# One list of fine steps for the start: attention of tiles 0 to 2 and the first layer of tiles 0 and 1

## The chip, the core and the metric

The kernel runs on one core of a Trainium2 chip. The time is that of the whole kernel on the device in microseconds (us), from inputs in HBM to the output in HBM; lower is better. Five queues run side by side, each in its own order: TensorE (PE, its weight loads as PEld), VectorE (DVE), ScalarE (ACT), GpSimd (POOL) and SyncE (SP), which here only issues DMAs. An instruction waits for semaphores of other queues, and all that stands behind it on its queue waits too.

## What is computed

Windowed causal attention over 4 batches, 8 heads, 576 positions and 64 columns, then two feed-forward blocks, all in float32:

```python
scores = scale * np.matmul(q, k.transpose(0, 1, 3, 2))
mask = (rel >= 0) & (rel < 64)                       # rel = row position - column position
scores = np.where(mask, scores, -1000000000.0)
scores = scores - np.max(scores, axis=-1, keepdims=True)
attn = np.exp(scores)
attn = attn / (np.sum(attn, axis=-1, keepdims=True) + 1e-09)
x = np.matmul(attn, v)                               # then laid out as 2304 tokens x 512
h = x @ moe_w_in;  x = (np.maximum(h, 0.0) + alpha * np.minimum(h, 0.0)) @ moe_w_out
h = x @ moe2_w_in; out = (h * (1.0 / (1.0 + np.exp(-h)))) @ moe2_w_out
```

The two inner widths are 2048. Weights arrive as 64-bit floats and are turned into float32 on DVE by bit operations.

## The kernel before

The 2304 tokens are cut into six tiles of 384. Attention is done in **items**: item n is two heads (128 rows of q and k) of one tile, four items a tile, so items 0 to 3 are tile 0, 4 to 7 tile 1, 8 to 11 tile 2. The steps of an item:

- S, `mm_s` (L178): 24 small matmuls into two PSUM banks, half "a" and half "b".
- softmax of a half (L188): three DVE instructions (L199) that add the mask and find the row minimum of the negated scores, then three ACT exponentials (L204).
- `rescale` (L210): DVE adds 1e-9 to the sums (L218), takes the reciprocal (L219) and multiplies the half by it in one instruction of 128x384 (L222).
- T, `mm_t` and `keep_t`: three PE transposes a half (L230), and one ACT copy of the bank to SBUF (L237).
- P, `mm_v` and `keep_v`: 24 matmuls with v (L247), an ACT copy rounded to the fast float format (high part, L256) and a DVE subtraction (low part, L257).

The first layer of a tile is 16 **chunks** f of 128 hidden rows. A chunk's weights are loaded by SP (L265) into one of four staging buffers, converted by three DVE instructions (L276, L279, L282), copied to a high part by ACT (L289) and subtracted to a low part by DVE (L290). M, `mlp_h1` (L338), is then 12 matmuls of 128x384 into bank 0 or 1 in turn; G, `mlp_g1`, is two ACT reads of that bank (L345, L346), and one tile-chunk later DVE joins the two (L356) and SP stores the result (L368). M of tile t needs the high and low parts of all four items of that tile.

The order of each queue is that in which the program calls the steps. Two places call them here. First a hand-written list, `START` (L20), whose words stand for coarse steps: `s3a` is S of item 3, softmax of its half a and rescale of the half b before it; `s3b` is softmax of half b and rescale of half a; `t3a` is transposes and copy; `p3` is P with both parts; `w`, `c`, `h` with a number load, convert or split all chunks up to that number; `M` and `G` are for tile 0. The list ends after M and G of four chunks of tile 0. Then the loop over t (L935) begins with t = 1: it works on the items of tile 2 and does M and G of chunk f for tiles 0 and 1 (tile 1 alone for f below 4), with the next chunks' load, conversion and split behind them. From t = 2 on one tile is left for each t, and a plan brings in the weights of later layers.

Attention has PSUM banks 2 to 7, given out in fixed turn (`turn_ab`, L123); the probabilities of items below 8 have eight rooms in fixed turn (L121), the transposed ones two rooms (L122).

Of the kernel before, what the change touches and what calls it, by code (L numbers as in the profile page):

```python
# [20 lines left out]
q0 w1 s0a q1 q2 s0b w2 s1a v0 s1b c1 q3 s2a v1 z s2b t0a t0b h1 q4 s3a p0 v2 w3 s3b t1a t1b c2 p1 v3 q5 s4a w4 s4b  # L21
t2a t2b h2 v4 p2 s5a w5 s5b t3a t3b v5 p3 c3 w6 s6a t4a t4b s6b M0 p4 h3 G0 c4 s7a t5a t5b s7b M1 p5 w7 G1 h4 t6a t6b
s8a M2 p6 s8b c5 G2 t7a t7b M3 p7 h5 G3
# [8 lines left out]
def attention_two_mlps(ctx, tc, q, k, v, w_in1, w_out1, alpha, w_in2, w_out2, out):  # L32
# [92 lines left out]
    def att_bank():  # L125
        return bank(turn_ab(), "pa")
# [51 lines left out]
    def mm_s(n):  # L178
        it = items[n]
        it["sc"] = [att_bank()[:, :HB * P].rearrange("p (b c) -> p b c", b=HB) for _ in range(2)]  # L180
        for jb in range(NB):
            o = jb * W
            for e in range(2):
                r = slice(e * W, (e + 1) * W)
                nc.tensor.matmul(it["sc"][jb % 2][side(jb, e), jb // 2, :], it["qT"][r, o:o + W],  # L185
                                 it["kT"][r, o:o + P], start=True, stop=True)

    def softmax(n, hf):  # L188

        it = items[n]  # L190
        t = n // NHP
        sc = it["sc"][hf]
        pr = room(turn_early() if n < EARLY else turn_pr(), [P, HB, P], F32, "pr")
        if hf == 0:
            it["sm"] = sml.tile([P, 2 * HB], F32, name="sm")

        nm = sml.tile([P, HB], F32, name="nm")
        for j in range(HB):
            nc.vector.tensor_tensor_reduce(  # L199
                out=pr[:, j, :], in0=sc[:, j, :],  # L200
                in1=mask[:, min(1, (t * NB + 2 * j + hf) % (S // W))].rearrange("p u w -> p (u w)"),
                scale=-scale, scalar=3.0e38, op0=ALU.add, op1=ALU.min, accum_out=nm[:, j:j + 1])
        for j in range(HB):
            nc.scalar.activation(out=pr[:, j, :], in_=pr[:, j, :], func=AF.Exp,  # L204
                                 bias=nm[:, j:j + 1], scale=-1.0, accum_out=it["sm"][:, hf * HB + j:hf * HB + j + 1])
        it[f"p{hf}"] = pr
        if hf and n >= NHP:
            load_qk(n + 2)

    def rescale(n, halves=(0, 1)):  # L210
        it = items.get(n)
        if it is None or halves[-1] in it.setdefault("scaled", set()):
            return
        it["scaled"].update(halves)
        c = slice(halves[0] * HB, (halves[-1] + 1) * HB)
        sm = it["sm"][:, c]
        rs = sml.tile([P, 2 * HB, 1], F32, name="rs")
        nc.vector.tensor_scalar_add(sm, sm, 1e-9)  # L218
        nc.vector.reciprocal(rs[:, c, :].rearrange("p b o -> p (b o)"), sm)  # L219
        for hf in halves:  # L220
            pr = it[f"p{hf}"]
            nc.vector.tensor_tensor(out=pr, in0=pr, in1=rs[:, hf * HB:(hf + 1) * HB, :].to_broadcast([P, HB, P]),  # L222
                                    op=ALU.mult)

    def mm_t(n, halves=(0, 1)):
        it = items[n]
        for hf in halves:
            pb = it[f"b{hf}"] = att_bank()
            for j in range(HB):
                nc.tensor.transpose(pb[:, j * P:(j + 1) * P], it[f"p{hf}"][:, j, :], ident)  # L230

    def keep_t(n, halves=(0, 1)):

        it = items[n]
        for hf in halves:
            pt = it[f"pt{hf}"] = room(turn_pt(), [P, HB, P], F32, "pt")
            nc.scalar.copy(pt, it[f"b{hf}"][:, :HB * P].rearrange("p (b c) -> p b c", b=HB))  # L237

    def mm_v(n):
        it = items[n]  # L240
        pb = it["pv"] = att_bank()
# [8 lines left out]
    def keep_v(n):  # L250
        pb = items.pop(n)["pv"]
# [4 lines left out]
        nc.scalar.copy(xh, pb[:, :TN])  # L256
        nc.vector.tensor_tensor(out=xl, in0=pb[:, :TN], in1=xh.bitcast(F32), op=ALU.subtract)  # L257
        xt[t, hp] = (xh, xl)
        if n >= NHP:
            load_v(n + 2)  # L260

# [5 lines left out]

    def to_f32(s, a=None):
        a = a or cv.tile([P, DM], U32, name="cva", tag="cv")
        for k in range(3):  # L270
            f32_step(s, a, k)
        return a.bitcast(F32)
# [27 lines left out]
    def plain_steps(key, src, f, base):  # L300
        def load():
            held[key, f] = stage(src, f)

        def convert():
            held[key, f] = to_f32(held[key, f])

        def split():
            a = held.pop((key, f))
            wh, wl = (wroom((base + 2 * f + i) % 64, [P, DM], F32R, key) for i in range(2))
            parts(a, wh, wl)  # L310
            wt[key, f] = (wh, wl)
        return load, convert, split
# [28 lines left out]
    def mlp_g1(t, f):  # L341
# [5 lines left out]
        join_g1()  # L347
        halves.append((t, f, a, g))

    halves = []  # L350

    def join_g1():
        if not halves:
            return
        t, f, a, g = halves.pop()
# [370 lines left out]


    in1 = [plain_steps("i1", w_in1, f, 0) for f in range(KF)]
    done = {}

    def upto(chunks, step, n):
        k = (id(chunks), step)
        while done.get(k, 0) < min(n, len(chunks)):
            chunks[done.get(k, 0)][step]()
            done[k] = done.get(k, 0) + 1

    ahead = set()
    for w in START.split():
        rests()
        x, n = w[0], int(w[1:].rstrip("ab") or 0)  # L740
        if x in "qv":
            (load_qk if x == "q" else load_v)(n)
        elif x == "z":
            alpha_in()
        elif x == "s":
            if w[-1] == "a":
                mm_s(n)
                softmax(n, 0)
                rescale(n - 1, (1,))
            else:  # L750
                softmax(n, 1)
                rescale(n, (0,))
        elif x == "t":
            hf = (int(w[-1] == "b"),)
            rescale(n, hf)
            mm_t(n, hf)
            keep_t(n, hf)
        elif x == "p":
            mm_v(n)
            keep_v(n)  # L760
        elif x in "wch":
            upto(in1, "wch".index(x), n)
        else:
            (mlp_h1 if x == "M" else mlp_g1)(0, n)
            ahead.add(n)
# [169 lines left out]
    for t in range(1, NTILE):  # L935
        for f in range(KF):
            rests()
            n = (t + 1) * NHP + f // 4
            if t + 1 < NTILE:
# [3 lines left out]
                elif f % 4 == 0:  # L943
# [4 lines left out]
                    if n > EARLY:  # L948
                        rescale(n)
                        mm_t(n)  # L950
                    if f:
                        keep_v(n - 1)
                    if n > EARLY:
                        keep_t(n)
# [4 lines left out]
                elif f % 4 == 2:  # L959
                    if n == EARLY:  # L960
                        for hf in ((0,), (1,)):
                            rescale(n, hf)
                            mm_t(n, hf)
                            keep_t(n, hf)
                    rescale(n + 1)
            for tt in ((0, 1) if t == 1 and f not in ahead else (t,)):
                mlp_h1(tt, f)
                mlp_g1(tt, f)
            if t == 1:
                upto(in1, 1, f + 4)  # L970
                upto(in1, 0, f + 7)
                upto(in1, 2, f + 3)
            else:
                hook((t - NTILE) * KF + f)
# [9 lines left out]
    join_g1()  # L984
# [99 lines left out]
```

## Time and profile before

| | us |
|---|---|
| median of three runs | 846.58 (846.17 to 849.41) |
| the profiled execution, whole | 849.5 |
| its span, first to last instruction | 847.7 |
| PE busy | 811.8 (96%) |
| DVE busy | 643.8 (76%) |
| ACT busy | 509.5 (60%) |

The page gives the busy time of each engine over the span; a PE time is modelled, so that a wait between two matmuls can hide in it. The granted TensorE clock is shown as a share of full speed: 1.00 is 2.4 GHz and 0.50 is 1.2 GHz, and its mean over the span is 0.979. The chain of waits is followed back from the last instruction; the timeline shows instructions with their start, their length, and in brackets the idle time of the engine before them.

### The profile page before, as it was taken

How to read it: one execution, taken by the hardware profiler on the slowest of the kernel's cores; microseconds unless marked ns; L12 is line 12 of the kernel's file. 1: busy time of each engine (PE TensorE's matmuls, PEld its weight loads, DVE VectorE, ACT ScalarE, POOL GpSimd, SP SyncE). 2: the span in 40 equal slices, each digit the busy share in tenths (PEclk: the TensorE clock that was granted, in tenths of full speed). 3: DMA queues.
4: the chain of work that ended last, by engine and by line, in shares of the span. 5: the costliest groups of instructions: out<-in, count | busy, mean ns of one | idle time of the engine just before them, and what ended most of it. 6: DMA issues, size and time to landing. Idle time of an engine off the chain costs nothing.

```text
span 847.7 us, 17779 instructions
## 1 busy us (share of the span) xinstructions
PE 811.8 (96%) x5976; PEld 791.5 (93%) x5976; DVE 643.8 (76%) x1603; ACT 509.5 (60%) x1327; POOL 79.8 (9%) x108
## 2 busy tenths in 40 slices
PE   4689999999999999999999999999989999999998
PEld 3579999989899999999999989999989999999998
DVE  5678886879888899798899786664765887756754
ACT  4576665666665577565577646645656575554553
POOL 1000000000000014023122000000000030421410
PEclk9599999999999999999999999999999999999999
DMA  8457737786867789898999597585878889659631
GB/s 260 151 171 235 237 113 235 238 279 222 276 204 254 235 269 194 252 305 216 321 240 250 182 329 261 207 287 187 255 264 265 283 176 328 142 110 318 118 61 57
DMA packets 136844, 190.47 MB, mean 225 GB/s; under 512 B 13872, under 2 KB 122928, under 8 KB 136752
## 3 DMA queue, kind: packets, MB, share of 16 engines
q1 hardware_dynamic: 124080, 172.02, 62.2%
q0 software_dynamic: 12672, 17.31, 12.4%
q8 instruction: 47, 0.77, 0.4%
q14 instruction: 45, 0.37, 0.1%
HBM read 110.11 MB, written 61.87 MB: 203 GB/s over the span
## 4 chain that ended last, share of the span: by engine, by line
PE 82%; DMA 7%; DVE 5%; ACT 3%; issue 2%; SPq 1%; ACTq 0%; DVEq 0%
PE acc L631 21%; PE h L338 20%; PE acc L436 19%; PE qa L515 9%; PE qd L515 5%; PE pa L247 3%; DMA w<-w_o 2%; PE pa L230 2%; PE qb L515 2%; PE pa L185 2%; ACT pr L204 1%; DMA g<-g 1%; DMA w_o<-ts 1%; DMA s<-in_moe_w_in_dram 1%; DMA kT<-in_k_dram 1%
## 5 line engine op out<-in xcount | busy, mean ns | idle before, releaser
L338 PE MATMUL h<-x,i 128*128 128x384 f32 x1152 | 208.5, 338 | 1.1 <-ACT g L346 1.1
L338 PEld LDWEIGHTS h<-x,i 128*128 128x128 f32 x1152 | 199.7, 189 | 3.0 <-ACT g L346 2.4
L631 PE MATMUL acc<-w,gh 128*128 128x256 f32 x984 | 145.6, 283 | 0.4 <-ACT gh L289 0.4
L436 PE MATMUL acc<-gh,o 128*128 128x384 f32 x672 | 143.6, 334 | 0.0
L631 PEld LDWEIGHTS acc<-w,gh 128*128 128x128 f32 x984 | 130.3, 192 | 0.7 <-ACT gh L289 0.6
L289 ACT CAST gh<-gf 128x384 fp32r<-128x384 f32 x168 | 85.8, 515 | 58.1 <-PE acc L436 51.5
L436 PEld LDWEIGHTS acc<-gh,o 128*128 128x128 f32 x672 | 118.9, 188 | 0.0
L515 PE MATMUL qa<-v,w 128*128 128x384 f32 x576 | 110.7, 340 | 4.8 <-ACT fk L520 2.9
L515 PEld LDWEIGHTS qa<-v,w 128*128 128x128 f32 x576 | 102.4, 191 | 6.2 <-ACT fk L520 4.0
L290 DVE TENSOR_TENSOR gl<-gf,gh 128x384 fp32r<-128x384 f32 x168 | 91.2, 553 | 15.7 <-ACT gh L289 11.7
L289 ACT CAST gh<-g 128x384 fp32r<-128x384 f32 x116 | 58.5, 514 | 48.9 <-PE acc L631 46.4
L631 PE MATMUL acc<-w,gl 128*128 128x256 f32 x492 | 86.8, 283 | 0.0
L345 ACT ACTIVATE a<-h 128x384 f32<-128x384 f32 x96 | 46.9, 489 | 66.1 <-PE h L338 50.9
L436 PE MATMUL acc<-gl,o 128*128 128x384 f32 x336 | 85.7, 335 | 0.1
L290 DVE TENSOR_TENSOR gl<-g,gh 128x384 fp32r<-128x384 f32 x116 | 62.5, 554 | 29.0 <-ACT gh L289 27.9
L395 POOL DMA_DIRECT2D gf<-gf x48 | 41.9, 904 | 416.5 <-DMA gf<-g 336.9
L356 DVE SCALAR_TENSOR_TENSOR g<-a,nalpha,g 128x384 f32<-128x384 f32 x96 | 58.6, 614 | 20.6 <-ACT g L346 20.5
L204 ACT ACTIVATE pr<-pr,nm 128x128 f32<-128x128 f32 x144 | 56.3, 395 | 26.4 <-DVE nm L199 26.3
L631 PEld LDWEIGHTS acc<-w,gl 128*128 128x128 f32 x492 | 71.3, 192 | 0.0
L290 DVE TENSOR_TENSOR w<-w 128x256 fp32r<-128x256 f32 x112 | 46.2, 418 | 20.2 <-ACT w L289 19.8
L436 PEld LDWEIGHTS acc<-gl,o 128*128 128x128 f32 x336 | 60.3, 188 | 1.1 <-DVE gl L290 1.0
L515 PE MATMUL qd<-v,w 128*128 128x384 f32 x288 | 58.7, 339 | 0.2 <-ACT fk L520 0.2
(89 smaller groups left out, 1108.6 us busy)
## 6 DMA issues: line engine op xcount, KB each, us to landing
g<-g SPq DMA_DIRECT2D x192, 192.0 KB, 4.3
gf<-g SPq DMA_DIRECT2D x96, 192.0 KB, 4.5
g<-c SPq DMA_DIRECT2D x96, 192.0 KB, 3.1
s<-in_moe_w_in_dram SPq DMA_DIRECT2D x32, 512.0 KB, 5.7
s<-in_moe_w_out_dram SPq DMA_DIRECT2D x32, 512.0 KB, 5.2
gf<-gf POOLq DMA_DIRECT2D x48, 192.0 KB, 5.0
w<-w_i SPq DMA_DIRECT2D x56, 128.0 KB, 4.1
w<-w_o SPq DMA_DIRECT2D x56, 128.0 KB, 3.1
```

The source lines that it names most:

```text
L185: nc.tensor.matmul(it["sc"][jb % 2][side(jb, e), jb // 2, :], it["qT"][r, o:o + W], it["kT"][r, o:o + P], start=True, stop=True)
L204: nc.scalar.activation(out=pr[:, j, :], in_=pr[:, j, :], func=AF.Exp, bias=nm[:, j:j + 1], scale=-1.0, accum_out=it["sm"][:, hf * HB + j:h ...
L247: nc.tensor.matmul(pb[r, jb * W:(jb + 1) * W], vt[:, jb // 2, r], it[f"pt{hf}"][:, j, side(jb, e)], start=True, stop=True)
L289: nc.scalar.copy(hi, src)
L290: lows.append(lambda: nc.vector.tensor_tensor(out=lo, in0=src, in1=hi.bitcast(F32), op=ALU.subtract))
L338: nc.tensor.matmul(h, w[:, kk, :], x, start=(kk == 0 and n == 0), stop=(kk == KD - 1 and n == 2))
L345: nc.scalar.activation(out=a, in_=h, func=AF.Relu, scale=-1.0)
L356: nc.vector.scalar_tensor_tensor(out=g, in0=a, scalar=nalpha[:, f:f + 1], in1=g, op0=ALU.mult, op1=ALU.add)
L395: nc.gpsimd.dma_start(out=o, in_=g1[u, b, c], accum_op=ALU.add)
L436: nc.tensor.matmul(o[i], w[:, a, i * P:(i + 1) * P], b, start=start and a == 0 and b is gh, stop=c == KH - 1 and b is gl, skip_group_check ...
L515: nc.tensor.matmul(o, w[:, a, k0], b, start=start and kk == 0 and n == 0, stop=kk == 1 and n == 2, skip_group_check=True)
L631: nc.tensor.matmul(acc2[u, v][i], a[:, i * P:(i + 1) * P], w[:, b, :], start=v in (A11, A12, S3) and c == 0 and a is gh and b == 0 and i != 1,
```

## The change

`START` becomes a list of single steps that covers all the work up to the loop's t = 2: attention of items 0 to 11, S and softmax of item 12, and M and G of all 16 chunks for tiles 0 and 1, written as `M0.5` (tile 0, chunk 5). The loop over t begins with 2. New letters: `m` the DVE part of softmax of a half, `e` its exponentials, `r` sum and reciprocal of a half, `s` its multiplication, `t` transposes, `k` the copy, `P`, `x`, `l` the P matmuls, high part and low part, `h`, `o` the high and low part of a chunk, `c0a` to `c0c` the three conversion steps, `G` the two ACT reads and `J` the join on DVE. M1.0 stands after M0.6, and from M0.7 on tiles 0 and 1 take turns.

Three more things change. The multiplication `s` of items 4 to 12 moves from one DVE instruction of 128x384 to three ACT instructions of 128x128 (L253). Banks, and rooms of items below 8, are taken from a list of free ones and returned when the last reader has been written, with two more rooms for the transposed halves. The loads of items from q14 on are called by the softmax of item 12 and later; those before stand in the list.

```diff
 START = """
-q0 w1 s0a q1 q2 s0b w2 s1a v0 s1b c1 q3 s2a v1 z s2b t0a t0b h1 q4 s3a p0 v2 w3 s3b t1a t1b c2 p1 v3 q5 s4a w4 s4b
...
+q0 q1 w0 q2 v0 w1 q3 v1 w2 q4 v2 w3 q5 v3 S0 S1 m0a m0b e0a c0a m1a e0b S2 m1b r0a e1a c0b r0b m2a e1b m2b r1a e2a r1b
...
+l1 w6 v6 m5a h2 s4a m5b P3 x2 o2 e5a l2 S6 r4b c3a x3 r5a e5b c3b S7 l3 s4b m6a s5a r5b m6b z M0.0 s5b m7a e6a m7b c3c
...
-    turn_pr = Turn(range(34, 38))
-    turn_early = Turn(list(range(28, 34)) + [36, 37])
-    turn_pt = Turn((38, 39))
-    turn_ab = Turn(range(2, 8))
+    AHEAD = 3 * NHP
+    ONACT = range(NHP, 13)
+    spare = {"pr": [*range(28, 34), 36, 37], "pt": [38, 39, 34, 35], "bank": list(range(2, 8))}
+    turn_pr, turn_pt = Turn(range(34, 38)), Turn((38, 39))
+
+    def take(kind, n=0):
+        if kind != "bank" and n >= EARLY:
+            return (turn_pr if kind == "pr" else turn_pt)()
+        return spare[kind].pop(0)
+
+    def give(kind, i, n=0):
+        if kind == "bank" or n < EARLY:
+            spare[kind].append(i)
...
-    def softmax(n, hf):
+    def peaks(n, hf):
...
+        give("bank", it["scb"][hf])
+
+    def exps(n, hf):
...
-        if hf and n >= NHP:
+        if hf and n >= AHEAD:
             load_qk(n + 2)
...
+    def scaled(n, hf):
+        it = items[n]
+        pr, rs = it[f"p{hf}"], it["rs"][:, hf * HB:(hf + 1) * HB, :]
+        if n in ONACT:
+            for j in range(HB):
+                nc.scalar.activation(out=pr[:, j, :], in_=pr[:, j, :], func=AF.Copy, scale=rs[:, j, :])
+        else:
+            nc.vector.tensor_tensor(out=pr, in0=pr, in1=rs.to_broadcast([P, HB, P]), op=ALU.mult)
...
+    def low_v(n):
+        it = items.pop(n)
+        xh, xl = xt[divmod(n, NHP)]
+        nc.vector.tensor_tensor(out=xl, in0=it["pv"][:, :TN], in1=xh.bitcast(F32), op=ALU.subtract)
+        give("bank", it["pvi"])
+        if n >= AHEAD:
             load_v(n + 2)
...
-    for t in range(1, NTILE):
+    for t in range(2, NTILE):
...
-            for tt in ((0, 1) if t == 1 and f not in ahead else (t,)):
-                mlp_h1(tt, f)
-                mlp_g1(tt, f)
-            if t == 1:
-                upto(in1, 1, f + 4)
-                upto(in1, 0, f + 7)
-                upto(in1, 2, f + 3)
-            else:
-                hook((t - NTILE) * KF + f)
+            mlp_h1(t, f)
+            mlp_g1(t, f)
+            hook((t - NTILE) * KF + f)
```

Two places show the new order. The first is ACT's queue while tile 0 is in attention. In it `pr_412` and `pr_427` of the kernel before are the halves of item 4's exponentials, and `pt` are copies of transposed halves, `pt_365` of item 1, `pt_447` and `pt_453` of item 2; `x` are high parts of items 1 and 2, and `i1` is a chunk. Before:

```order
L237 COPY pt_365<-pa_361 128x384
L256 CAST x_384<-pa_371 128x384
L204 ACTIVATE pr_412,sm_413<-pr_412,nm_414 128x128 x3
L204 ACTIVATE pr_427,sm_413<-pr_427,nm_428 128x128 x3
L237 COPY pt_447<-pa_443 128x384
L237 COPY pt_453<-pa_449 128x384
L289 CAST i1_455<-cva_367 128x512
L256 CAST x_476<-pa_463 128x384
```

The same engine at the same stage after, where `pr_307` and `pr_318` are item 3, `pr_419` is item 4, and the `pt` rows are items 0 (`pt_316`, `pt_360`), 1 and 2:

```order
L281 COPY pt_316<-pa_303 128x384
L229 ACTIVATE pr_307,sm_327<-pr_307,nm_308 128x128 x3
L229 ACTIVATE pr_318,sm_327<-pr_318,nm_319 128x128 x3
L281 COPY pt_360<-pa_312 128x384
L361 CAST i1_373<-cva_218 128x512
L281 COPY pt_384<-pa_323 128x384
L281 COPY pt_400<-pa_333 128x384
L281 COPY pt_417<-pa_376 128x384
L303 CAST x_424<-pa_386 128x384
L229 ACTIVATE pr_419,sm_428<-pr_419,nm_420 128x128 x3
```

Before, the two copies of item 2 stand behind both exponentials of item 4, and the other items follow in the same pattern; after, the first copy of item 0 stands ahead of item 3's exponentials, and four more copies stand together ahead of item 4's.

The second place is DVE where the first chunks of layer 1 run. `s64` is a staging buffer, `cva` a converted chunk, `i1` its low part, `g` a join, `x` a low part, `sm` and `rs` sums and reciprocals. Before, around chunk 4:

```order
L222 TENSOR_TENSOR pr_791<-pr_791,rs_850 128x384
L276 TENSOR_SCALAR cva_854<-s64_507 128x512
L279 SCALAR_TENSOR_TENSOR cva_854<-s64_507,cva_854 128x512
L282 SCALAR_TENSOR_TENSOR cva_854<-s64_507,cva_854 128x512
L356 SCALAR_TENSOR_TENSOR g_757<-a_756,nalpha_107,g_757 128x384
L257 TENSOR_TENSOR x_902<-pa_888,x_901 128x384
L290 TENSOR_TENSOR i1_910<-cva_854,i1_909 128x512
```

After, between the low parts of chunks 4 and 5 (`cva_676` is chunk 5, `cva_768` chunk 6 and `cva_773` chunk 8):

```order
L365 TENSOR_TENSOR i1_720<-cva_674,i1_719 128x512
L245 TENSOR_SCALAR sm_711<-sm_711 128x3
L246 RECIPROCAL rs_744<-sm_711 128x3
L413 SCALAR_TENSOR_TENSOR g_737<-a_736,nalpha_107,g_737 128x384
L332 SCALAR_TENSOR_TENSOR cva_676<-s64_437,cva_676 128x512
L245 TENSOR_SCALAR sm_711<-sm_711 128x3
L246 RECIPROCAL rs_744<-sm_711 128x3
L326 TENSOR_SCALAR cva_768<-s64_511 128x512
L326 TENSOR_SCALAR cva_773<-s64_717 128x512
L413 SCALAR_TENSOR_TENSOR g_763<-a_762,nalpha_107,g_763 128x384
L365 TENSOR_TENSOR i1_771<-cva_676,i1_770 128x512
```

The conversion of a chunk, one block of three before, is spread between sums, joins and other chunks, and the first step of chunk 8 stands ahead of the low part of chunk 5.

## Rows read from the trace of the kernel before

**Rows 1.** Windows; columns: length, PE, PEld, DVE, ACT, POOL busy (instructions), clock, DMA, GB/s.
```profile
0.00:43.06 43.06, 24.60 (x295) 20.15 (x296) 25.92 (x122) 22.11 (x87) 3.10 (x20) 0.70 0.63 202
43.06:69.64 26.58, 23.15 (x265) 20.53 (x264) 21.45 (x90) 20.74 (x76) 0.00 (x0) 0.97 0.62 180
69.64:133.74 64.10, 63.40 (x502) 60.72 (x500) 50.21 (x123) 39.07 (x109) 0.00 (x0) 1.00 0.66 209
133.74:847.70 713.96, 700.68 (x4921) 690.05 (x4920) 546.25 (x1271) 427.61 (x1056) 76.69 (x88) 0.99 0.77 229
```

**Rows 2.** Chain of waits, P2, S5, T3, then M; columns: start, length, what.
```profile
31.67 1.66 PE pa L247 x24
33.33 1.49 PE pa L185 x24
34.82 1.47 PE pa L230 x6
36.30 2.14 issue
...
43.06 2.82 PE h L338 x12
```

**Rows 3.** Timeline of ACT in the same cycle; columns: start, length, instruction, idle before.
```profile
29.95 0.40 ACT L204 ACTIVATE pr<-pr,nm 128x128 f32<-128x128 f32 x1 [0.25 <-DVE nm L199]
...
31.12 0.83 ACT L237 COPY pt<-pa 128x384 f32<-128x384 f32 x2
31.85 0.62 ACT L289 CAST i<-cva 128x512 fp32r<-128x512 f32 x1
```

**Rows 4.** Chain of waits in the loop's t = 1, at full clock.
```profile
84.42 0.37 ACT a L345
...
85.22 8.60 PE h L338 x48
93.82 0.85 PE pa L247 x24
94.67 0.81 PE pa L185 x24
95.48 0.81 PE pa L230 x6
```

**Rows 5.** Timeline of DVE, first chunk and halves.
```profile
6.03 0.29 DVE L199 CUSTOM_DVE_ANT_0 pr<-pa,mask 128x128 f32<-128x128 f32 x1 [6.03 <-PE pa L185]
...
12.02 0.28 DVE L199 CUSTOM_DVE_ANT_0 pr<-pa,mask 128x128 f32<-128x128 f32 x1
...
12.66 0.17 DVE L218 TENSOR_SCALAR sm<-sm 128x3 f32<-128x3 f32 x1
...
13.06 0.56 DVE L222 TENSOR_TENSOR pr<-pr,rs 128x384 f32<-128x384 f32 x1
13.54 0.42 DVE L276 TENSOR_SCALAR cva<-s 128x512 uint32<-128x512 uint32 x1
13.99 0.69 DVE L279 SCALAR_TENSOR_TENSOR cva<-s,cva 128x512 uint32<-128x512 uint32 x1
14.72 0.69 DVE L282 SCALAR_TENSOR_TENSOR cva<-s,cva 128x512 uint32<-128x512 uint32 x1
15.33 0.28 DVE L199 CUSTOM_DVE_ANT_0 pr<-pa,mask 128x128 f32<-128x128 f32 x1
...
19.80 0.69 DVE L290 TENSOR_TENSOR i<-cva,i 128x512 fp32r<-128x512 f32 x1 [1.28 <-ACT i L289]
...
27.13 0.56 DVE L257 TENSOR_TENSOR x<-pa,x 128x384 fp32r<-128x384 f32 x1 [0.88 <-ACT x L256]
```

**Rows 6.** Chain of waits: the join, and a load.
```profile
3.56 5.22 DMA kT<-in_k_dram
...
67.72 0.62 DVE g L356
```

**Rows 7.** DMA issues of the page: KB each, median us to landing.
```profile
s<-in_moe_w_in_dram SPq DMA_DIRECT2D x32, 512.0 KB, 5.7
```

More of the change, by code (lines that the diff above doesn't have):

```diff
@@ L179, in mm_s @@
         it = items[n]
-        it["sc"] = [att_bank()[:, :HB * P].rearrange("p (b c) -> p b c", b=HB) for _ in range(2)]
+        it["scb"] = [take("bank") for _ in range(2)]
+        it["sc"] = [bank(i, "pa")[:, :HB * P].rearrange("p (b c) -> p b c", b=HB) for i in it["scb"]]
         for jb in range(NB):
@@ new lines, in over @@
+    def over(n, halves):
+        it = items[n]
+        c = slice(halves[0] * HB, (halves[-1] + 1) * HB)
+        sm = it["sm"][:, c]
+        if "rs" not in it:
+            it["rs"] = sml.tile([P, 2 * HB, 1], F32, name="rs")
+        nc.vector.tensor_scalar_add(sm, sm, 1e-9)
+        nc.vector.reciprocal(it["rs"][:, c, :].rearrange("p b o -> p (b o)"), sm)
+    def scaled(n, hf):
+        it = items[n]
+        pr, rs = it[f"p{hf}"], it["rs"][:, hf * HB:(hf + 1) * HB, :]
[4 more added lines that the diff above has]
+            nc.vector.tensor_tensor(out=pr, in0=pr, in1=rs.to_broadcast([P, HB, P]), op=ALU.mult)
+        it.setdefault("scaled", set()).add(hf)
@@ L210, in rescale @@
     def rescale(n, halves=(0, 1)):
         it = items.get(n)
-        if it is None or halves[-1] in it.setdefault("scaled", set()):
+        if it is None or halves[-1] in it.get("scaled", ()):
             return
[L214 to L219, printed above, removed]
+        over(n, halves)
@@ L227, in mm_t @@
         for hf in halves:
[L228 removed]
+            it[f"bi{hf}"] = take("bank")
+            pb = it[f"b{hf}"] = bank(it[f"bi{hf}"], "pa")
             for j in range(HB):
                 nc.tensor.transpose(pb[:, j * P:(j + 1) * P], it[f"p{hf}"][:, j, :], ident)
+            give("pr", it[f"pi{hf}"], n)
     def keep_t(n, halves=(0, 1)):
@@ L248, in mm_v, with high_v @@
                                  it[f"pt{hf}"][:, j, side(jb, e)], start=True, stop=True)
-    def keep_v(n):
-        pb = items.pop(n)["pv"]
+        for hf in range(2):
+            give("pt", it[f"pti{hf}"], n)
+    def high_v(n):
         t, hp = divmod(n, NHP)
@@ L297, in attention_two_mlps, with load_1, convert_1, high_1 @@
     held = {}
[L300 to L312, printed above, removed]
+    def load_1(f):
+        held["i1", f] = stage(w_in1, f)
+    def convert_1(f, k):
+        if k == 0:
+            held["i1", f] = held["i1", f], cv.tile([P, DM], U32, name="cva", tag="cv")
+        f32_step(*held["i1", f], k)
+    def high_1(f):
+        a = held["i1", f] = held["i1", f][1].bitcast(F32)
+        wt["i1", f] = tuple(wroom(2 * f + i, [P, DM], F32R, "i1") for i in range(2))
+        nc.scalar.copy(wt["i1", f][0], a)
+    def low_1(f):
+        h, o = wt["i1", f]
+        nc.vector.tensor_tensor(out=o, in0=held.pop(("i1", f)), in1=h.bitcast(F32), op=ALU.subtract)
     def combos(b11, b12, b21, b22, t, k, minus=False):
@@ L983, in attention_two_mlps @@
                     split_g1(f - KF + 3)
-    join_g1()
+    while halves:
+        join_g1()
     store_g1(0)
```

131 lines of the change are left out of this document (61 added, 70 removed).

## The prediction

> **What bounds the kernel now.** I read the windows first, cut at three marks of the chain of waits: the first M, the last wait of the loop's t = 1, and the S that opens t = 2 [rows 1]. From 133.74 us on nothing is moved: after the list the SP queue has the same loads and stores in the same order, and PE is busy for 700.68 of 713.96 us there. So only the first 133.74 us can change, and the question is when S of item 13 starts.
>
> What must PE do until then? At full clock a run of four M takes 8.60 us, so one is 2.15; P is 0.85, S 0.81, and T of both halves 0.81 [rows 4]. There are 32 M (68.8), 12 P (10.2), 13 S (10.5) and 12 T (9.7): 99.2 us, before and after. The other 34.5 us are what can be won. Up to 43.06 us PE does 4 P, 7 S and 5 T, 13.1 us of that work, and so loses 30. From 43.06 to 69.64 it does 6 M, 4 P, 3 S and 4 T, 21.9 us in 26.58, and loses 4.7. From 69.64 to 133.74 the rest is 64.1 us in 64.10: nothing is lost.
>
> The first loss is a ring of three engines. In the chain P of item 2, S of item 5 and T of item 3 follow each other, 1.66, 1.49 and 1.47 us, and then PE stands for 2.14 before the next P [rows 2]. The profile calls that gap "issue", but ACT's timeline shows the wait: the copies start at 31.12, behind the exponentials of item 4 that wait for DVE at 29.95, and P starts as the first copy is done [rows 3]. One item costs 6.76 us, and no M can be done until four items are through. The matmuls also take twice as long as at full clock (S 1.49 against 0.81): the mean granted clock up to 43.06 is 0.70 [rows 1], the low level of 1.2 GHz for much of it.
>
> **What the change does to the first M.** The list splits the ring: DVE, ACT and PE each get work of another item while one waits. I add DVE's queue up to the low part of item 3 (`l3`), the last thing M0.0 needs. Neighbouring starts give the prices [rows 5]: three minima 0.64 (12.02 to 12.66), sum and reciprocal 0.40, multiplication 0.48, the conversion steps 0.45, 0.73 and 0.61; a chunk's low part is 0.69 busy and an item's 0.56, each taken 0.08 less for the overlap that the multiplication shows (0.56 busy, 0.48 apart). Ahead of `l3` stand 12 halves of minima (7.7), 11 of sums (4.4), 8 multiplications (3.8), three chunks and two steps converted (6.5), 3 chunk lows (1.8) and 3 item lows (1.4): 25.6 us. DVE's first instruction follows S of item 0 at 6.03 [rows 5], since the first four DMAs are the same. That would put `l3` at 31.6. One wait is sure: `c0a` is now third on DVE and needs the first chunk, which is issued behind q1. The bytes up to it are those that stood up to kT of item 1 before (q0, q1 and 512 KB of weights), and that landed at 8.78 (3.56 plus 5.22 [rows 6]). So DVE stands from 7.3 to 8.8, and `l3` starts at 33.1 and ends at 33.6. PE in the same time has 13.1 us of work (4 P, 8 S, 4 T), about 26 at half clock. Its last five steps are S5, P2, P3, S6 and S7, 7.8 us at half clock. S5 takes the bank that the first copy of item 3 frees, and on ACT that copy stands behind the high part of chunk 1, whose conversion DVE ends at 24.5 (6.03, 1.5 of waiting and 17.0 of queue); with that high part and two copies it is done at about 26. Both engines arrive at **34 us** for M0.0, against 43.06: 9 us won. The later loads hide: q6 and q7 are issued behind `c0c` and `c1c` at some 20 and 25 us, land about 5 us later and are read by S6 and S7 at 31 and 32.6. Bounds: 31.6 if the wait for `c0a` is nothing and PE is fast, and 37 if each load lands a chunk's 5.7 us late once [rows 7].
>
> **From M0.0 to the end of the list.** Left are 32 M, 8 P, 5 S and 8 T: 86.1 us of PE. Before it was the same work and 90.7 us. The rest is waits, and I look at the stretch with most, M0.0 to M1.0. PE has 7 M, 4 P, 2 S, 4 T: 23.3 us. DVE has 4 halves of minima (2.6), 4 of sums (1.6), 11.8 of conversion (six chunks and two steps), 4 chunk lows (2.4), 4 item lows (1.9) and 7 joins of 0.55 (0.62 less the overlap [rows 6]): 24.2. ACT has 7 G (0.75 each, two reads 0.37 apart [rows 4]), 5 chunk highs (0.62 busy [rows 3], 0.53 with the overlap), 8 copies and 4 item highs (0.37 to 0.47), 5 halves of exponentials (1.17, from 29.95 to 31.12 for three [rows 3]) and the 5 multiplications that moved here. Those have no row. From above, three exponentials with their sums read out cost 1.17; from below, one ACT pass over all 384 columns costs 0.37. I take 0.92, nearer to the exponential, the only ACT instruction of 128x128 with an operand per partition, less what the reading out of sums may cost. ACT then has 23.5. So three queues are level, within 1 us.
>
> With the three level, single waits show. One I can price: the first step of chunk 8 stands eleven DVE instructions behind the last step of chunk 4, whose staging buffer its load must wait for. Between them DVE has 4.3 us, the load takes 5.7 [rows 7], so DVE stands 1.4; the low part of chunk 5 is directly behind, and M0.5 waits for it, some 1.9 with the hop to ACT and back. I add 0.6 before M1.0 (the low parts of items 6 and 7 are its last operands), 0.4 for M0.0 at rising clock and 1.2 for the tail, where P8, T11 and the last M stand behind short chains on ACT. Sum: 4.1. The list would end at 34.1 + 86.1 + 4.1 = **124.3**, against 133.74: 9.4 us earlier. Ends of the waits: 0.5, since the stretch from 69.64 lost nothing, and 13, if the loss of 4.7 in 26.58 us [rows 1] is had in all 73 us in which attention and M are mixed.
>
> Off PE: DVE gives up 18 multiplications of 0.48, 8.6 us, and ACT takes 18 of 0.92, 16.6. ACT was busy for 81.92 us up to 133.74 (22.11 + 20.74 + 39.07 [rows 1]); 98 in 124 still fits. The list of free banks costs nothing by itself; what it hides is the turn, by which a matmul waits for the oldest bank even if another is free. Moving the loads q8 to q13 and v8 to v13 puts them into SP's queue ahead of chunks 9 to 13; SP then waits for the rooms that T of items 4 to 6 leaves, which is at M0.5 and before.
>
> **A rule that speaks against it.** The multiplication costs DVE 0.48 a half [rows 5], and ACT's nearest row makes it 0.92 [rows 3]. The Trainium skill, page "ScalarE: Activation LUTs", section "Rules for kernel authors", says to use VectorE, not ScalarE, for a multiplication. By that rule the 18 halves cost 8 us more engine time than they save. By the rows it depends on who is last: with the five on DVE, M0.0 to M1.0 would hold 26.6 us of DVE and 18.9 of ACT against 23.3 of PE. Where ACT is the last one, the rule is right, which is the second rival.
>
> **The rivals.**
> 1. PE never waits behind M0.0. For it: the loop of t = 1 lost nothing. Against: DVE has 24.2 us there for PE's 23.3. It starts at 33.0 with 1.0 of waits: 120.1, 13.6 won, 833.0.
> 2. ACT is last. If a moved half costs 1.17 and G stands behind the exponentials that wait for DVE, bank 0 or 1 comes free late and each of 14 M up to M1.6 waits some 0.4: 5.6 more, 3.8 won, 842.8.
> 3. Slower: SP's line. The loads of chunks 8 to 12 are issued behind q8, v8, q9 and v9, which wait for PE's transposes, while PE waits for these chunks. If each of the five comes 3 us late (5.7 to land, 2.7 of DVE work in between) DVE and PE stand 15 us: 5.6 lost, 852.2. It decides from 9.4 us of such waits on. Against: T of items 4 to 6 is due at M0.5, about when the buffer for chunk 9 comes free anyway.
> 4. The change only moves the waits: the half clock and the first loads set the start as before, M0.0 comes at 42, and the rest as forecast: 1.4 won, 845.2.
>
> **How the numbers follow.** The profiled execution took 849.5 with a span of 847.7; the same sum there gives 838.3 of span and 840.1. It lies 2.9 above the median of 846.58, so I take the difference to the median: 846.6 - 9.4 = **837.2**. Chances: the forecast (834 to 841) 0.55, rival 1 0.19, rival 2 0.14, rival 4 0.07, rival 3 0.05. The range of 8 in 10 reaches from 831.5 (M0.0 at 32, hardly a wait) to 843.5. A measurement of this kernel can tell about 0.5% from no change, 842.3 and 850.8. Faster by more: the forecast, rival 1 and 0.08 of rival 2, which straddles the line: 0.82. Within: the other 0.06 of rival 2, and rival 4: 0.13. Slower: rival 3, 0.05.
>
> **What would show it.** In the profile after, the first M should start near 34 us, and S of item 13 (24 matmuls, directly behind the last M of tile 1) near 124. Gaps on PE should be short, the longest ahead of M0.5 with the low part of chunk 5 as its releaser. The ACT multiplication should be near 0.3 apart. If the first M starts near 34 and the list ends past 130, the level queues were the mistake; if M0.0 is past 39, the start was. The stretch behind the list should keep its 714 us; if it doesn't, the loads of later weights have moved against the work, which I hold for nothing.

## The result and the profile after

Four runs of the changed kernel have a median of 838.31 us (836.46 to 840.68), against 847.91 (846.17 to 849.41) for four of the kernel before: a ratio of 0.9889, 95% interval 0.9852 to 0.9926. That is 9.6 us won; 9.4 were forecast. In two repeats, each beside the kernel before on its own chip, it is 7.9 and 11.3 (e0 and e13 below). The profiled execution is the longest of the four, 840.68 us with a span of 838.9.

Here are the windows of the changed kernel, cut at the first M, at the first M of tile 1, and at S of item 13. They answer to [rows 1] and have its columns.

```profile
0.00:31.80 31.80, 19.35 (x312) 14.92 (x312) 23.66 (x123) 23.06 (x93) 3.10 (x20) 0.99 0.92 294
31.80:57.28 25.48, 24.33 (x254) 22.35 (x253) 21.18 (x72) 23.48 (x77) 0.00 (x0) 0.95 0.73 226
57.28:120.64 63.36, 62.79 (x496) 59.33 (x493) 40.80 (x133) 49.18 (x159) 0.00 (x0) 1.00 0.48 160
120.64:838.90 718.26, 702.58 (x4920) 690.06 (x4920) 546.12 (x1269) 427.31 (x1056) 76.78 (x88) 1.00 0.77 230
```

The first M starts at 31.80 where it stood at 43.06, and the list ends at 120.64 instead of 133.74: 13.1 us are won there, against one profiled execution of the kernel before, which took 849.5 us, more than its median. The last row takes 4.3 of them back: the stretch behind the list, in which no instruction was moved, is 718.26 us long and was 713.96.

The ring of [rows 2] is gone. VectorE and ScalarE are busy for 23.66 and 23.06 of the first 31.80 us, where they had 25.92 and 22.11 in 43.06. The clock is granted at 0.99 there instead of 0.70. The timeline of TensorE (start, length, instruction, idle before and its releaser) shows the longest gap between 15 us and the first M:

```profile
27.75 0.49 PE L206 MATMUL pa<-kT,qT 64*64 64x128 f32 x8
30.47 1.41 PE L206 MATMUL pa<-kT,qT 64*64 64x128 f32 x24 [2.23 <-DVE sm L245]
31.80 0.69 PE L391 MATMUL h<-x,i 128*128 128x384 f32 x1
```

S of item 7 waits for 2.23 us. The clock is then granted at 0.67 during that S, at 0.53 in the 2.7 us behind it, in M0.0, and at 1.00 from 34.5 us on. The profile names a sum on VectorE as the releaser, of which S reads nothing. What S reads are the keys of item 7, and their load (issue on SyncE, then the time to landing) lands at 30.3, just ahead of it:

```profile
24.23 0.43 SPq L175 DMA_DIRECT2D kT<-in_k_dram  x1
DMA to landing us min/median/max: 6.1/6.1/6.1
```

The first M follows S without a gap, so this load sets its start. On VectorE the low part of item 3, the last operand of M0.0, ends 0.2 us before it, but only the eleventh matmul of M0.0 reads it. Two waits of VectorE stand out in its timeline:

```profile
9.05 0.43 DVE L326 TENSOR_SCALAR cva<-s 128x512 uint32<-128x512 uint32 x1 [2.16 <-DMA s<-in_moe_w_in_dram]
...
31.03 0.55 DVE L309 TENSOR_TENSOR x<-pa,x 128x384 fp32r<-128x384 f32 x1
...
35.58 0.17 DVE L126 TENSOR_SCALAR nalpha<-alpha_sb 128x16 f32<-128x16 f32 x1 [2.47 <-DMA alpha_sb<-in_moe_alpha_dram]
```

The first is the wait for the first weight chunk, forecast at 1.5. The second was not forecast: the small load of alpha is issued at `z`, behind the seventh weights, and the chain of waits of this kernel gives it 6.39 us, from 29.16 on. The table has the marks of every profile that is told of below.

| kernel | first M | S of item 13 | behind it | span | time, median |
|---|---|---|---|---|---|
| before | 43.06 | 133.74 | 714.0 | 847.7 | 845.8 to 847.9 in four comparisons |
| after | 31.80 | 120.64 | 718.3 | 838.9 | 838.31 |
| after, again (e0) | 31.82 | 119.66 | 716.8 | 836.5 | 837.98 |
| after, again (e13) | 31.46 | 118.83 | 715.9 | 834.7 | 835.37 |
| multiplication on VectorE (e1) | 30.71 | 120.87 | 714.1 | 835.0 | 837.95 |
| alpha early (e2) | 30.73 | 117.83 | 716.2 | 834.0 | 835.52 |
| alpha early, first conversion step later (e5) | 31.55 | 118.66 | 718.5 | 837.2 | 837.38 |
| more on ScalarE (e8) | 30.46 | 121.82 | 714.1 | 835.9 | 836.72 |
| banks in turn (e4) | 32.28 | 118.79 | 711.0 | 829.8 | 831.73 |
| banks in turn (e12) | 32.91 | 119.11 | 712.0 | 831.1 | 833.90 |
| banks in turn, alpha early (e11) | 31.97 | 117.80 | 712.3 | 830.1 | 831.51 |
| old order, free lists and ScalarE (e6) | 43.93 | 146.81 | 716.6 | 863.4 | 866.25 |
| old order, free lists alone (e10) | 39.61 | 130.68 | 715.6 | 846.3 | 848.28 |
| before, TensorE kept busy (e7) | 38.55 | 131.85 | 712.9 | 844.7 | 845.45 |

### The profile page after: what moved, and what is told of

It is laid out like the page before. It is cut to its first block, busy times and chain, and to the rows that moved or that the text cites. A ratio compares the mean times of both kernels' runs of the same rounds, so it can differ in the third digit from the quotient of the medians.

```text
span 838.9 us, 17786 instructions
## 1 busy us (share of the span) xinstructions
PE 809.0 (96%) x5976; PEld 786.7 (94%) x5976; DVE 631.8 (75%) x1593; ACT 523.0 (62%) x1381; POOL 79.9 (10%) x108
## 4 chain that ended last, share of the span: by engine, by line
PE 79%; DMA 9%; DVE 7%; ACT 3%; issue 1%; SPq 1%; ACTq 0%; DVEq 0%
PE acc L688 20%; PE acc L493 19%; PE h L391 18%; PE qa L572 10%; PE qd L572 5%; DMA w<-w_o 3%; PE qb L572 2%; DMA s<-in_moe_w_in_dram 2%; PE pa L293 2%; PE pa L272 2%; PE pa L206 1%; DMA g<-g 1%; DMA kT<-in_k_dram 1%; ACT pr L229 1%; DMA alpha_sb<-in_moe_alpha_dram 1%
## 5 line engine op out<-in xcount | busy, mean ns | idle before, releaser
L340 DVE TENSOR_TENSOR gl<-g,gh 128x384 fp32r<-128x384 f32 x116 | 62.8, 556 | 29.7 <-ACT gh L339 28.6
L413 DVE SCALAR_TENSOR_TENSOR g<-a,nalpha,g 128x384 f32<-128x384 f32 x96 | 59.0, 615 | 23.3 <-ACT g L399 22.0
L339 ACT CAST w<-w 128x256 fp32r<-128x256 f32 x112 | 43.5, 402 | 24.7 <-DMA w<-w_o 20.4
```

The lines of the kernel that those rows point to most:

```text
L339: nc.scalar.copy(hi, src)
L340: lows.append(lambda: nc.vector.tensor_tensor(out=lo, in0=src, in1=hi.bitcast(F32), op=ALU.subtract))
L413: nc.vector.scalar_tensor_tensor(out=g, in0=a, scalar=nalpha[:, f:f + 1], in1=g, op0=ALU.mult, op1=ALU.add)
```

## The experiments

Theory: the order of the list gains, since it breaks the ring; the move of the multiplication and the free lists serve that order. Rivals: the clock, granted low while TensorE stood, is most of it; or the free lists gain by themselves.

**The changed kernel again (e0).**

> The changed kernel, unchanged, for a second profile of what lies behind the list. The list (S of item 13) should again start near 120.6 us. Behind it the first profile took 718.3 us, 4.3 more than the 714.0 of the kernel before. Theory A: that is the chance of the DMAs, whose landing sets the few PE waits there; then this profile gives another number between 712 and 719. Theory B: the new list shifts the later loads against the work; then it is again 717 to 719.

Measured: 837.98 us (835.37 to 838.53), ratio 0.9911 (0.9882 to 0.9940). Item 13 starts at 119.66 and 716.8 us follow. The loss behind the list is there again, with 2.8 us instead of 4.3: another number inside the range of theory A, and just below that of theory B.

**The old order with the free lists and the multiplication on ScalarE (e6).** The order of steps is that of the kernel before; the free lists and the ScalarE multiplication of items 4 to 12 are those of after. The rooms for transposed probabilities are two, as before.

```diff
-q0 q1 w0 q2 v0 w1 q3 v1 w2 q4 v2 w3 q5 v3 S0 S1 m0a m0b e0a c0a m1a e0b S2 ...
+q0 w0 S0 m0a e0a q1 q2 m0b e0b r0a s0a w1 S1 m1a e1a r0b s0b v0 m1b e1b r1a ...
...
-    spare = {"pr": [*range(28, 34), 36, 37], "pt": [38, 39, 34, 35], "bank": list(range(2, 8))}
+    spare = {"pr": [*range(28, 34), 36, 37], "pt": [38, 39], "bank": list(range(2, 8))}
```

> The order of the kernel before, word for word on PE and on SP, written as a list of fine steps in the changed kernel: banks and rooms are still given out as they come free (two rooms for transposed halves instead of four), and the multiplication of items 4 to 12 is on ACT. Theory (the order pays, the rest only makes it possible): the list ends within 3 us of 133.7 and the time is 845 to 850. Rival (the free lists and ACT's share pay by themselves): it ends below 130 and the time is below 843.

Measured: 866.25 us (863.41 to 868.27), ratio 1.0249 (1.0214 to 1.0284); item 13 only at 146.81. Neither side had this. The timeline of ScalarE, in one cycle of the ring, shows why:

```profile
35.03 0.40 ACT L230 ACTIVATE pr<-pr,nm 128x128 f32<-128x128 f32 x1 [1.33 <-DVE nm L218]
...
36.20 0.97 ACT L254 ACTIVATE pr<-pr,rs 128x128 f32<-128x128 f32 x3
...
38.22 0.97 ACT L254 ACTIVATE pr<-pr,rs 128x128 f32<-128x128 f32 x3
39.10 0.83 ACT L282 COPY pt<-pa 128x384 f32<-128x384 f32 x2
```

Two halves of exponentials and two multiplications stand ahead of the copies that P waits for. P starts at 39.65 after 3.53 us of waiting, and the cycle is 8.15 us (the P before is at 31.50) where [rows 2] had a wait of 2.14 and a cycle of 6.76. In the ring ScalarE is a link, and the move makes the link longer. The clock, too, is lower from the first M to item 13, 0.95 where e10 below has 0.99; how much of the loss that is, isn't separated.

**The old order with the free lists alone (e10).** The same, with the multiplication on VectorE.

```diff
-    ONACT = range(NHP, 13)
+    ONACT = ()
```

> The order of before word for word, the multiplication of every half by the reciprocals on VectorE as before; of the change only the free lists of banks and buffers and the two more rooms for transposed probabilities stay. Theory (the order of the list is what gains; giving out by free lists changes nothing by itself): the item-13 scores start at 133 to 135 us and the time is 846 to 849. Rival (the free lists gain by themselves, since a group no longer waits for the bank that is next in turn): item 13 at 131 or earlier and 845 or less. Against the kernel with the old order and the multiplications of items 4 to 12 on ScalarE (item 13 at 146.8) it also tells what that move costs in the old order: theory 12 to 14 us.

The two more rooms that the expectation speaks of are not in this kernel: it has two, like e6. Measured: 848.28 us (845.03 to 850.12, ten runs), ratio 1.0020 (1.0003 to 1.0037). In this one profile item 13 starts at 130.68, so the mark falls to the rival and the time to the theory. Its clock differs: 0.85 up to the first M, against 0.70 [rows 1], and the waits of P in the ring are those of before (2.81, 2.17 and 2.14 us). The free lists, under the old order, are worth nothing in time. Beside e6 it prices the move in that order: 18 us for the whole kernel, 16 at item 13, above the 12 to 14 expected.

Two parts of the change stand in neither kernel, the two more rooms and the earlier loads. With the old order the rooms could change nothing: on TensorE P of each item stands ahead of T of the next, so both rooms have been read when the next copy can start. And in the kernel before no wait of TensorE, VectorE or ScalarE between 13.7 and 133.7 us has a load as its releaser.

**The kernel before with TensorE kept busy (e7).** Idle transposes of the identity in bank 1, whose results nobody reads.

```diff
                 mm_s(n)
+                if n == 3:
+                    fill(24)
...
             mm_t(n, hf)
+            if hf == (1,) and 1 <= n <= 3:
+                fill(14)
```

> The kernel before with idle work added on TensorE, whose results nobody reads: 24 transposes of the identity behind the scores of item 3 and 14 behind the second transposes of items 1, 2 and 3, to keep the granted clock at 1.00 where before it was 0.50 (17.6 to 44.8 us). In the ring of waits TensorE's links are 1.66 + 1.49 + 1.47 = 4.6 of each 6.8 us at half clock. Theory A (half of what the list gained is the clock, which fell because TensorE stood still): with the clock at 1.00 the first matmul of the first layer starts at 35 to 39 us instead of 43.1 and the time is 839 to 845. Theory B (the ring is bound by VectorE and ScalarE, and faster links only wait longer): the start stays at 42 to 44 and the time at 845 to 849, though the clock is 1.00. If the clock stays at 0.50 all the same, the start is at 43 to 46 and nothing is told.

Measured: 845.45 us (842.85 to 848.39), ratio 0.9983 (0.9966 to 0.9999). These are its windows, cut at the first M and at item 13:

```profile
0.00:38.55 38.55, 27.11 (x360) 23.27 (x361) 24.31 (x119) 22.23 (x87) 3.10 (x20) 1.00 0.72 226
38.55:131.85 93.30, 87.87 (x765) 82.09 (x763) 73.19 (x215) 59.68 (x184) 0.00 (x0) 0.98 0.62 195
```

And this is a cycle of its chain of waits (start, length, what; the matmuls named h are the idle ones):

```profile
30.32 1.13 PE pa L252 x24
31.45 0.82 PE pa L185 x24
32.26 0.81 PE pa L230 x6
33.07 1.53 PE h L235 x14
34.60 1.45 issue
36.05 1.15 PE pa L252 x24
```

The clock is 1.00 up to the first M, and that M comes at 38.55, 4.5 us earlier: theory A holds for the start, while the time misses its 845 by 0.45 and lies in the range of theory B. The ring itself remains: its links run at full clock, P still waits (1.45 us, behind the idle work), and a cycle takes 5.73 us instead of 6.76. Of the 4.5 us only 1.9 are left at item 13, since PE then waits for copies and halves of the next items, and the time shows less still. So of the 11.3 us by which the change starts M earlier, at most 4.5 belong to the clock, and the clock alone would have been worth 1 to 2 us in all. The theory stands: the order is the gain.

**The multiplication back on VectorE, in the new order (e1).** The edit is that of e10, in the changed kernel.

> One part undone: the multiplication by the reciprocal of items 4 to 12 goes back from ACT to DVE, 18 halves of 0.48 us there instead of 0.9 on ACT. Theory (DVE is the fullest queue of the three): between M0.0 and M1.0 DVE gets 2.4 us more, PE waits for chunks, the list ends 2 to 4 us later, 123 to 125, and the time is 2 to 4 us longer than that of the changed kernel. Rival (ACT is the last of the three, the multiplication belongs on DVE): the list ends at 120.6 or up to 2 us earlier.

Measured: 837.95 us (836.74 to 839.67), ratio 0.9918 (0.9889 to 0.9947): the same as e0 beside it. Item 13 starts at 120.87: the theory's mark, 123 to 125, is missed, and the rival's by 0.3. The stretch behind the first M tells why.

```profile
30.71:120.87 90.16, 86.40 (x747) 80.43 (x745) 70.65 (x223) 59.56 (x183) 0.00 (x0) 1.00 0.53 177
```

VectorE has 70.65 of 90.16 us, ScalarE 59.56; the changed kernel had 61.98 and 72.66 in 88.84. The stretch is 1.3 to 2.8 us longer than in the three profiles of the changed kernel, but the first M stands about 1 us earlier, since the keys of item 7 landed earlier here (29.7 us). So the move is worth 0.2 to 2.0 us by the mark of item 13 and 1.3 to 2.8 by the stretch, and nothing that the time shows.

**Five more half passes on ScalarE (e8).** They multiply by 1.0 and add nothing else.

```diff
+            if (n, hf) in ((5, 1), (6, 0), (6, 1), (7, 0), (7, 1)):
+                for j in range(HB):
+                    nc.scalar.activation(out=pr[:, j, :], in_=pr[:, j, :], func=AF.Copy, scale=1.0)
```

> The changed kernel with five more half passes on ScalarE (a multiplication by 1.0 of three blocks each, about 0.9 us a half, 4.5 in all) for items 5 to 7, in the stretch from the first matmul of the first layer to that of the second tile. Theory (ScalarE, busy 23.5 of 25.5 us there, is at its limit): that stretch grows from 25.5 to 28.5 to 30, item 13 comes at 122.5 to 125. Rival (ScalarE's work there waits and can wait): it grows by under 1.5 and item 13 stays below 122.

Measured: 836.72 us (835.81 to 837.63, two runs), against 835.37 (831.96 to 836.50) for the unchanged one beside it (e13); the times overlap, so the profile has to tell.

```profile
30.46:58.86 28.40, 24.88 (x255) 22.96 (x253) 22.81 (x77) 27.36 (x98) 0.00 (x0) 0.94 0.71 228
```

From the first M to that of tile 1 it is 28.40 us instead of 25.48 (24.0 and 24.5 in e0 and e13), with ScalarE busy for 27.36; the wait ahead of the third M is 2.54 us, "ACT g" its releaser. Item 13 comes at 121.82. Both marks of the theory are just missed; of the rival's, the growth of under 1.5 us is far off and item 13 below 122 is met. Of the 4.4 us added, 1.2 to 3.0 arrive by the mark of item 13, and 2.5 to 4.0 by the stretch from the first M, which is earlier here (91.4 us against 88.8, 87.8 and 87.4). ScalarE is near its limit there, as forecast, with some 2 to 3 us of room at most.

**The load of alpha early (e2).** It goes behind `v3`, the fourth load of v (the expectations of e5 and e11 call it the fifth); the negation stays at `z`.

```diff
-... w3 q5 v3 S0 S1 m0a ...
+... w3 q5 v3 y S0 S1 m0a ...
```

> One wait taken away: the 8 KB load of alpha is issued behind v3, some 15 us earlier on the SP queue, while its one DVE instruction keeps its place. In the changed kernel DVE stands 2.5 us for that load at 33 us. Theory (DVE is behind in this stretch and PE waits for its chunks): the waits ahead of M0.3 and M0.5 (0.46 and 0.69 us) go, M1.0 and the end of the list come 1 to 2 us earlier, 118.6 to 119.6. Rival (ACT, busy 0.94 to 0.98 of the time from 32 to 57 us, is last): the end of the list moves by less than 0.5.

Measured: 835.52 us (833.52 to 836.33), ratio 0.9882 (0.9849 to 0.9915), 2.5 below e0 beside it. The intervals overlap, and the unchanged kernel itself came to 835.37 in e13, so the time doesn't settle it. The wait of VectorE is gone; item 13 starts at 117.83, which is 2.8, 1.8 and 1.0 us earlier than in the three profiles of the changed kernel. Of that, 0.7 to 1.1 us lie ahead of the first M, where the keys of item 7 landed earlier (29.7 us). From the first M to item 13 it is 87.1 us against 88.8, 87.8 and 87.4: by that stretch the wait for alpha is worth 0.3 to 1.7.

**Alpha early and the first conversion step two steps later (e5).** The load of alpha is placed as in e2.

```diff
-... m0a m0b e0a c0a m1a e0b S2 m1b r0a ...
+... m0a m0b e0a m1a e0b S2 m1b c0a r0a ...
```

> The changed kernel with the load of alpha behind the fifth load of v, and the first sums of the first weight chunk placed two steps later on VectorE (after the masks of items 0 and 1). Theory (VectorE has no gap from 9 to 33 us, so 2 us in which it stood for the first weights come off M0.0): M0.0 at 29 to 30 us and item 13 at 116 to 117.5 against 117.8 with the early load alone; time 833 to 835. Rival (that wait only moves to a mask, and something else is last at M0.0): item 13 at 117.8 or later, 835.5 or more.

Measured: 837.38 us (832.26 to 839.00), ratio 0.9873 (0.9837 to 0.9909): the theory falls. On VectorE the wait of 1.99 us for the first chunk (e2) only moves to two waits for S, of 0.74 and 1.17. And the first M is no earlier; TensorE's timeline names what is late:

```profile
26.87 0.98 PE L208 MATMUL pa<-kT,qT 64*64 64x128 f32 x24 [0.35 <-DMA kT<-in_k_dram]
30.62 1.00 PE L208 MATMUL pa<-kT,qT 64*64 64x128 f32 x24 [2.78 <-DMA kT<-in_k_dram]
31.55 0.70 PE L393 MATMUL h<-x,i 128*128 128x384 f32 x2
```

S of item 7 waits for its keys, loaded at `q7`. In e13, where nothing is changed, it waits 2.75 us for the same load. It is so in every profile with the new order and the list of banks: S of item 7 starts 0.1 to 0.2 us after these keys land (at 30.3, 30.1 and 30.4 us in the three of the changed kernel, 29.7 in e1 and e2, 30.5 here, 29.4 in e8), and the first M follows S at once. VectorE's low part of item 3 doesn't hold it. In e8 M0.0 starts half a microsecond ahead of that instruction:

```profile
29.53 1.00 PE L206 MATMUL pa<-kT,qT 64*64 64x128 f32 x24 [1.31 <-DMA kT<-in_k_dram]
30.46 1.31 PE L394 MATMUL h<-x,i 128*128 128x384 f32 x6
31.01 0.55 DVE L312 TENSOR_TENSOR x<-pa,x 128x384 fp32r<-128x384 f32 x1
```

**Banks in a fixed turn, in the new order (e4).**

```diff
...
-        return spare[kind].pop(0)
+        return turn_ab() if kind == "bank" else spare[kind].pop(0)
```

> The changed kernel with its six banks of the list given out in a fixed turn again (first in, first out, whatever is free), pr buffers still from the free list. Theory (the list was ordered for banks that come free out of turn: a bank of G is held until its eviction while a bank of T comes free within 1 us): PE waits 2 to 6 us more between M0.0 and item 13, which then stands at 122 to 126 against 119.7 to 120.6, and the time is 840 to 844. Rival (banks come free nearly in the order they are taken): item 13 within 1 us of 120, time within 1.5 of 838.

Measured: 831.73 us (830.05 to 834.55), ratio 0.9820 (0.9794 to 0.9846). This contradicts the theory: the fixed turn isn't slower but 6.2 to 6.6 us faster than the changed kernel had been so far. At item 13 it is only 0 to 1.9 us ahead; the rest lies behind the list, 711.0 us. The next two put it beside the changed kernel on one chip.

> The changed kernel with banks in fixed turn once more, beside the changed kernel itself on the same chip. Theory A (the turn is worth 1 to 2 us in the list and nothing behind it; the other 4 to 5 us were how the late loads fell): item 13 within 1 us of 119, the stretch behind it 714 to 718, the time within 2.5 us of the changed kernel's. Theory B (the turn moves something that lasts to the end): 711 to 713 behind item 13 again and the time 5 to 7 us below the changed kernel's.

> The changed kernel unchanged, for its stretch behind the list on the same chip as the kernel with the fixed turn. If that stretch belongs to the change: 716 to 718.5 us as in both profiles so far (kernel before: 714.0), and 836 to 839 in all. If it only varies: below 715, or waits at other places than the five of both profiles.

Measured: 833.90 us (832.86 to 835.45), ratio 0.9859 (0.9835 to 0.9884), and for the changed kernel 835.37 (831.96 to 836.50), ratio 0.9864 (0.9836 to 0.9891). In time they can't be told apart there. In the profiles the stretch behind the list is 712.0 and 715.9 us. So for the turn the time goes with theory A and the stretch with theory B, and the stretch of the unchanged kernel lies between its two alternatives: what the turn is worth stays open.

**What the stretch behind the list waits for.** At some 650 us, ahead of the last stage, TensorE waits for VectorE, which itself stood for a copy that goes through DRAM (`g<-g`). These are lines of the two timelines in the changed kernel:

```profile
647.45 0.87 PE L688 MATMUL acc<-w,gs 128*128 128x256 f32 x6
648.09 1.20 DVE L663 TENSOR_TENSOR s<-g 128x384 f32<-128x384 f32 x2 [3.99 <-DMA g<-g]
650.75 1.83 PE L688 MATMUL acc<-w,gs 128*128 128x256 f32 x12 [2.43 <-DVE gs L340]
652.38 2.12 PE L572 MATMUL qa<-v,w 128*128 128x384 f32 x6
```

TensorE at the same place with the fixed turn (e4):

```profile
641.81 0.87 PE L688 MATMUL acc<-w,gs 128*128 128x256 f32 x6
643.76 1.70 PE L688 MATMUL acc<-w,gs 128*128 128x256 f32 x12 [1.07 <-DVE gs L340]
645.30 1.21 PE L572 MATMUL qa<-v,w 128*128 128x384 f32 x6
```

The window behind that wait in the changed kernel:

```profile
650.00:655.00 5.00, 4.25 (x22) 4.25 (x23) 2.74 (x6) 2.94 (x8) 0.00 (x0) 0.71 0.73 271
```

And with the fixed turn (e4):

```profile
643.00:648.00 5.00, 4.24 (x32) 4.24 (x33) 3.75 (x9) 3.29 (x8) 0.00 (x0) 1.00 0.89 302
```

In the changed kernel the wait is 2.43 us and the clock then falls to half: six matmuls take 2.12 instead of 1.21 us. With 1.07 us of waiting it stays at 1.00. Such waits come at a few places of the program (in the changed kernel near 365, 490, 600 to 618 and 650 us), and whether they come and how long they are varies. Those over 0.15 us from 284 us on add up to 6.7 us before, 9.1, 8.8 and 8.1 in the three profiles of the changed kernel, and 5.6, 5.8 and 7.5 in the three with the fixed turn; a fall of the clock costs an estimated 1.6 more each (the first 24 matmuls of M take 5.99 us behind a fall in e5, 4.43 without one in e13). Before had two falls ahead of the last microseconds, after two, e0 and e13 one, the three with the fixed turn none. Less these waits and falls the stretch is 704.8 to 706.4 us in these six profiles, so the difference between list and turn lies there. In the kernel before it is 704.1: of its 4.3 us to the first profile after, some 2.4 are waits, and the rest I can't place. Why these copies land later in one kernel than in another I can't show: the stretch lies between 711.0 and 718.5 us in kernels that do the same there, and with the old order between 712.9 and 716.6.

**Both together (e11).**

> The changed kernel with banks of the list given out in fixed turn and with the load of alpha behind the fifth load of v. Theory (both gains are in the list and add up): item 13 at 116 to 117.5 (118.8 with the turn alone, 117.8 with the early load alone), the stretch behind it 711 to 714, the time 828 to 831.5. Rival (what the turn seemed to gain lay in the stretch behind the list, 711.0 us in that one profile against 716 to 718, and is how the late loads happened to fall): the stretch is 715 to 718 again and the time 833 to 836.

Measured: 831.51 us (830.56 to 832.33), ratio 0.9825 (0.9805 to 0.9844), item 13 at 117.80, 712.3 us behind it. It is the best version here with e4, 3.9 us below the changed kernel on the same chip. The stretch behind the list is as the theory has it; item 13 and the time lie just above its ranges. The early load takes 1.0 to 1.3 us off the turn's list, less than the 1.3 to 2.8 expected.

## Why the prediction was right

- **The bound.** It held that only the time up to item 13 can change and that a ring is broken there. The ring is gone, and e7 and e10 show that neither the clock nor the free lists replace the order. The difference of 9.6 us is the forecast one, but that it is so near is luck: two errors cancel, a list that ends 3.7 us earlier than forecast (120.6 for 124.3) and a stretch behind it that is 4.3 longer.
- **First M at 34.** It came at 31.5 to 31.8, within the bounds, but not by what was named. The step that failed is "the later loads hide": the keys of item 7 were issued when forecast, at 24.2, but took 6.1 us to land, and TensorE was through with S of item 6 at 28.2 and stood for them. VectorE comes in only ahead of that load, by the conversion step `c1c` (it ends at 23.3) behind which it is issued. `l3` is not what the start waits for (e8). Its queue was near all the same, 31.03 for 33.1: the wait for the first chunk was longer (2.16 for 1.5), the sums with their reciprocal shorter (0.29 us apart, not 0.40), and the first instruction came at 5.54, not 6.03. TensorE at half clock, taken over from the kernel before, was wrong too; it was granted 0.97 to 1.00.
- **Waits of 4.1 behind the first M.** They were 2.7 after (88.84 less 86.1), 1.7 and 1.3 in the repeats. The largest term, 1.9 ahead of M0.5, is 0.69 after and 0.4 to 0.5 in the repeats; VectorE waits 0.52 there, not 1.4. The 0.4 for M0.0 at rising clock were some 1.2 after (24 matmuls in 5.58 us, 4.43 in e13). Not in the sum: VectorE's 2.47 for alpha (1.22 and 1.85 in the repeats), which e2 prices at 1.0 to 2.8 us by the mark of item 13 and 0.3 to 1.7 by the stretch behind the first M. I had given that load no price, though `z` was moved.
- **The multiplication.** 0.92 us a half was taken; after, three take some 1.0 from first start to last end, and the next instruction can start 0.88 after the first. ScalarE was busy for 23.48 us of the stretch to M1.0 (23.5 forecast). VectorE had 21.18 (24.2 forecast), so the three queues are not level: ScalarE is fuller than VectorE. The rule of the Trainium skill (page "ScalarE: Activation LUTs", section "Rules for kernel authors"), to multiply on VectorE, agrees in the price, 0.88 against 0.48 [rows 5]. In time it is without effect in the new order (e1) and right by 18 us in the old (e6 and e10), the lower clock of e6 included.
- **Free banks.** I said that the list costs nothing and hides the turn. Put back, the turn costs nothing: from the first M to item 13 it is 86.5 and 86.2 us in e4 and e12, against 88.8, 87.8 and 87.4 with the list. What the list was to hide isn't there; ahead of the first M the turn is up to 1.5 us later (32.3 and 32.9).
- **"The tail keeps its 714 us".** This step failed: 718.3, 716.8 and 715.9 us. I had read 713.96 as a property of unchanged code; it holds waits for copies and falls of the clock, which vary by several us with the execution and the version. It cost 2 to 4 us of the 13 to 15 won in the list.
- **The rivals.** The first, PE never waits, came near in the list itself (S at 118.8 to 120.6, 120.1 named there). The second, ScalarE last, is bounded by e8: 4.4 us more on it cost 1.2 to 3.0 by the mark and 2.5 to 4.0 by the stretch. The third, SP's line, appears only as the keys of item 7, and the fourth is refuted by the first M.

## What to carry to other kernels

Where three engines pass one item round, look at the order first: here finer steps gained 8 to 11 us, and faster matmuls in the old ring 1 to 2. Ask of each moved instruction whether its new engine is a link of the ring, since the same move cost nothing in one order and 18 us in the other. A stretch whose code is unchanged still has waits for transfers in it, and a forecast should give it the spread of several profiles. A load that is called hidden needs its own sum: when it is issued, how long it takes, and when its reader could start at the earliest (the keys of item 7). A tiny load moved with a step (alpha) counts like a large one when a queue stands for it: its 8 KB took 6.4 us to land, the 512 KB of a chunk 5.9.

## What was unexpected of the hardware

A gap of TensorE does not by itself tell whether the clock falls: S of item 7 waited 2.23 us after, and the clock was 0.53 in the 2.7 us of M0.0 behind it; in e13 it waited 2.75 us and the granted clock stayed at 1.00 up to the first M and on to item 13. And ScalarE's multiplications, 0.39 us each, start 0.29 us apart or a little more.
